# Attention in front of a mixture of experts: the gate weights' cast, the copies out of shared PSUM banks, the offsets' loads and batch 1's v and scaling are placed anew

## The chip, the core and the metric

The kernel runs on one core of a Trainium2 chip. TensorE (PE), VectorE (DVE), ScalarE (ACT), GpSimd (POOL) and SyncE (SP) each take their own instructions in order and wait for one another by semaphores; DMA queues move data between the device memory and the on-chip memories SBUF and PSUM. The metric is the device time of one execution in microseconds (us); the median of the runs counts.

## What is computed

q, k and v have 8 batches, 8 heads, 576 rows and 64 columns. Cut to what matters:

```
q_s = exp(q - max(q, -1)); q_s /= q_s.sum(-1)              # per row
k_s = exp(k - max(k, 2));  k_s /= k_s.sum(2)               # per column, over the sequence
kv  = einsum('bhsd,bhse->bhde', k_s, v)
x   = einsum('bhsd,bhde->bhse', q_s, kv)  -> (4608, 512)    # heads side by side
logits = x @ w_gate + modality_bias[modality_id]           # 8 experts
e   = argmax(logits);  g = softmax(logits)[e]
out[e == i] = g * (relu(x[e == i] @ w1[i]) @ w2[i])        # 512 -> 1024 -> 512
```

With these inputs the modality's bias decides the expert, so each modality has one: two experts, called A and B, are used.

## The kernel before

The program is planned in Python: every piece of work is an `Op` with a cost for each engine that may do it, a rank, and the pieces it depends on. `Plan.order` plays the plan with those costs and writes the instructions in the planned order; each engine then takes its row in that order on the chip, whatever the real times are. `pl.later(o, first)` makes o wait for first in the plan. `Plan.fill` adds unread products (L1498) to PE's row where the plan has PE idle, up to a planned time called `quiet`, until which one PSUM bank is also kept for them.

Batch by batch the attention runs so. SP loads q, k and v into five staging buffers `st` (L414), which are freed by the last work that reads them. ACT takes exp of q (L855) and k (L888), DVE sums q's rows (L861) and inverts the sums (L873), and the scaling (L877, five pieces: four of two column groups and one of one) writes scaled q as bf16 in `eq`; it runs on DVE for batches 0 to 2 and on GpSimd for the others. v is cast to bf16 in two halves (L898): by ACT in batches 0 and 1, by ACT or GpSimd later. PE forms kv in two halves (L990, 18 products each). DVE inverts k's sums (`kinv`, L1017, L1020) and writes the scaled kv as a block diagonal (`kvbd`, L1026, four instructions). PE multiplies scaled q by a permutation (`perm`, L906 on DVE) that sorts rows of the two modalities apart (L1066, 18 products in five groups), ACT or DVE evicts that (`et`, L1078, L1080), and PE multiplies by kvbd (L1105, 20 products in five groups, each group one PSUM bank).

From such a bank the results go to the window of x where A's rows or B's rows stand next: for each 64 rows one copy for A and one for B (L1136, `put`), 18 copies per batch. The windows' offsets are read from `offp` into registers (L1040, a load on each engine that copies). The tuple `copier` says who copies: in batches 0 and 1, A's copies are ACT's and B's are DVE's; in batches 2 and 5 DVE does both, in the others ACT.

When a batch's copies are in place, a pass of A and a pass of B (256 rows each) can run on PE: logits (L1174), first layer (L1241, 32 products of 256 columns, relu by ACT or DVE, L1208, L1210), second layer (L1254, 16 products of 512 columns), gates, `y_sb` (L1214, L1216) and a store by GpSimd (L1219). The logits need the gate weights in bf16, `wg_sb` (L526, cast by DVE from `wg_f`). The experts' weights `W` are loaded by GpSimd's queue (L534, L545) among SP's loads. The rows' places in the output come from comparisons on DVE (`hhi` L725, twelve of `hlo` L713), products of digits on GpSimd (`hv` L737, six) and 36 products on PE (L754), read by DVE as `lst` and `idx` (L766, L768). Copies from batch 3 on wait for those 36 products, since they overwrite their operands.

Of the kernel before, what the change touches and what calls it, by code (L numbers as in the profile page):

```python
# [16 lines left out]
ACT = mybir.ActivationFunctionType  # L17
# [202 lines left out]
def on_act(n):  # L220
    return {"ACT": (0.065 + n / 1200, 0.27 + n / 1200)}


def on_dve(n, rate=1, port=False):
    return {"DVE": (0.065 + n / 960 / rate, 0.28 + n / 960 / rate, port)}


def on_pool(n, per=1.0):
    return {"POOL": (0.07 + n * per / 1000, 0.2 + n * per / 1000, True)}
# [13 lines left out]
def kernel(  # L243
# [13 lines left out]
    B, H, S, Dh = q.shape  # L257
# [5 lines left out]
    NJ = S // 64  # L263
# [21 lines left out]
    pl = Plan()  # L285
# [152 lines left out]
    def load_batch(b):  # L438
        for nm in "qkv":
            load_one(nm, b)  # L440
# [36 lines left out]
    ahead = next(i for i, x in enumerate(transfers) if isinstance(x, str))  # L477
    for b in transfers[:ahead]:
        load_batch(b)
    l_wg = pl.op({"DMA": (0.4, 3.5)}, load_wg, rank=0)  # L480


    key = sb([P, 2], FP32, "key")
# [24 lines left out]
    def experts(_):  # L508
# [16 lines left out]
    wg_c = pl.op(  # L525
        on_dve(32), lambda _: nc.vector.tensor_copy(out=wg_sb, in_=wg_f), [l_wg, c_dve2], rank=11  # L526
    )
# [299 lines left out]
    final, edge, scaled_q = [], {}, []  # L827
# [7 lines left out]
        )  # L835

    started = {"a": False, "b": False}
    filled, perms = {}, []

    copier = [("ACT", "DVE")] * 2 + [(e, e) for e in ("DVE", "ACT", "ACT", "DVE", "ACT", "ACT")]  # L840

    def attention(b):
# [3 lines left out]
        R = 10.0 * b  # L846
# [79 lines left out]
        for (h, n), e in zip(halves, eqx):  # L926
# [5 lines left out]
                    rank=R + 1,  # L932
# [4 lines left out]
        for h, n in halves:  # L937
# [5 lines left out]
                    rank=R + 2,  # L943
# [5 lines left out]
        nq = []  # L949
        for j0, n in groups:  # L950
            n_ = n * HG * Dh
            ncost = on_pool(n_, 1.88)
            if b <= 2:
                ncost = on_dve(n_, 1, True)
            nq.append(
                pl.op(
                    ncost,
                    norm_q(j0, n),
                    [iq] + nq[:1],
                    rank=R + 1,  # L960
                    takes=[] if nq else [eqb],
                    uses=[eqb, qib, bq] if nq else [qib, bq],
                )
            )
# [2 lines left out]
            for o in (o_slot, o_bsel):  # L967
                pl.later(o, nq[-1])
        vcost = {**on_act(S * 2), **on_pool(S * 2, 0.95)}
        if b < 2:  # L970
            vcost = on_act(S * 2)
        cv = []
        for hp in range(2):
# [5 lines left out]
                    rank=R + 0.5,  # L979
# [21 lines left out]
        for hp in range(2):  # L1001
# [5 lines left out]
                    rank=R + 2,  # L1007
# [25 lines left out]
        o_ki = pl.op({"DVE": (0.45, 0.55)}, kinv_run, kvo, rank=R + 2, takes=[kib], uses=kvp)  # L1033
        o_kb = pl.op({"DVE": (1.24, 1.4)}, kvbd_run, [o_ki, c_pool2], rank=R + 2, takes=[kvb], uses=[*kvp, kib])

        ets, win, firsts = [], [], []
        av = {}

        def load_off(e):
# [8 lines left out]

        los = [
            pl.op(  # L1050
                {e: (1.2 if e == "ACT" else 0.6, 1.3)},
                load_off,
                [o_off] + filled.get(b - 2, [])[-2:],
                rank=R + (2.2 if b == 1 else 0.2),
            )
            for e in dict.fromkeys(copier[b])
        ]
        for gi, (j0, nj) in enumerate(groups):
            sbuf = Buf(r_ps)
            w = nj * 64  # L1060
# [13 lines left out]
            def ev(e, j0=j0, nj=nj, sbuf=sbuf):  # L1074
# [11 lines left out]
                rank=R + 3,  # L1086
# [9 lines left out]
                rank=R + 3,  # L1096
# [3 lines left out]
        for gi, (j0, nj) in enumerate(groups):  # L1100
            xbuf = Buf(r_ps)

            def s2(_, j0=j0, nj=nj, xbuf=xbuf):
# [13 lines left out]
                rank=R + 4,  # L1117
# [4 lines left out]
            for jj in range(nj):  # L1122
                for side in range(2):

                    def put(e, jj=jj, j0=j0, nj=nj, side=side, xbuf=xbuf):
# [19 lines left out]
                        if b == B - 1:  # L1145
# [1 line left out]

                    before = win[-2] if len(win) > 1 else filled[b - 1][side - 2] if b else None

                    across = win[-1 - 2 * side] if j0 + jj == NJ - 1 else None  # L1150
                    same = before and before.costs.keys() == {copier[b][side]}
                    win.append(
                        pl.op(
                            on_dve(256) if copier[b][side] == "DVE" else on_act(256),
                            put,
                            [o3, o_id if b >= 3 else None, *los, None if same else before, across],
                            rank=R + 4,
# [2 lines left out]
                    )  # L1160
                    if same:
                        pl.follow(win[-1], before)
        filled[b] = win


    L = sb([P, NSL, E], FP32, "L")
# [319 lines left out]
    for b in range(B):  # L1486
        attention(b)
# [3 lines left out]
        gs = [ffn(side, *p, rank=2.0 * i + side) for side, p in enumerate((pa, pb))]  # L1491
    ffn_rest(gs, 2.0 * i + 0.7)

    quiet = 32.0

    def unread(_):

# [158 lines left out]
```

## Time and profile before

| | us |
|---|---|
| median of 3 runs | 201.58 |
| lowest, highest | 200.18, 202.13 |
| profiled execution | 200.07 |
| its span, first to last instruction | 198.4 |

The profiled execution has 1.67 us around its span. Times below are from the span's start. In a timeline row the first number is the start, the second the time until the last of the merged instructions ended; what stands in brackets is idle time of the engine ahead of it, and what ended it.

### The profile page before, as it was taken

To read this page: it belongs to the slowest core of one execution; us is meant where nothing else is said; L and a number is where in the kernel's file an instruction comes from. 1 tells how busy PE (TensorE), PEld (TensorE's weight loads), DVE (VectorE), ACT (ScalarE), POOL (GpSimd) and SP (SyncE) were. 2 spreads that over 40 slices of the span, in tenths; PEclk is the share of its full clock that TensorE was granted. 3 is DMA by queue.
4 is the path that set the end of the run, shared out by engine and by line. 5 is a ranking of instruction groups with operands and counts; after the bars stand their busy time and mean duration, and the time that the engine had idled before them with its cause. 6 is when DMAs were issued, how large, how long until landed. Compare 5 with 4: busy or idle time off the path is not lost.

```text
span 198.4 us, 5000 instructions
## 1 busy us (share of the span) xinstructions
PE 181.1 (91%) x1757; PEld 123.9 (62%) x1757; DVE 152.3 (77%) x406; ACT 124.5 (63%) x246; POOL 94.8 (48%) x119
## 2 busy tenths in 40 slices
PE   0979986789999999999999999999899999999970
PEld 0435474457596666758685867586757756766740
DVE  3879998789999997958878999856788656655750
ACT  2765889679494786999998996699898000000000
POOL 7089303944540369598496329893112311331241
PEclk9999999699999999999999999999999999999998
DMA  5999999999999999998979941120202102211202
GB/s 189 355 280 259 390 294 247 397 287 211 212 336 407 399 389 340 295 377 267 386 288 280 398 165 55 56 109 0 109 0 107 76 33 106 106 56 53 96 32 90
DMA packets 18588, 42.33 MB, mean 213 GB/s; under 512 B 1913, under 2 KB 1913, under 8 KB 18562
## 3 DMA queue, kind: packets, MB, share of 16 engines
q1 hardware_dynamic: 13344, 28.33, 40.2%
q0 software_dynamic: 5200, 13.64, 23.8%
q8 instruction: 14, 0.23, 0.4%
q14 instruction: 12, 0.10, 0.1%
q10 hardware_dynamic: 18, 0.04, 0.1%
HBM read 36.75 MB, written 9.70 MB: 234 GB/s over the span
## 4 chain that ended last, share of the span: by engine, by line
PE 58%; DVE 17%; ACT 8%; issue 4%; DMA 4%; SPq 3%; POOL 2%; DVEq 1%; ACTq 0%
PE ps L1254 24%; PE ps L1241 23%; DVE xs L1136 5%; ACT xs L1136 4%; DMA wg_f<-in_moe_w_gate_dram 4%; PE ps L990 3%; DVE eq L877 3%; DVE xs L713 3%; PE ps L1105 2%; PE ps L1066 2%; SPq L414 2%; DVE kvbd L1026 2%; PE ps L1174 2%; DVE own L861 1%; POOL eq L877 1%
## 5 line engine op out<-in xcount | busy, mean ns | idle before, releaser
L1241 PE MATMUL ps<-xs,W 128*128 128x256 bf16 x576 | 68.3, 273 | 0.0
L1254 PE MATMUL ps<-W,hT 128*128 128x512 bf16 (+1 forms) x296 | 67.2, 378 | 0.0
L1219 POOL DMA_INDIRECT out_dram<-y_sb,idx x36 | 36.1, 1002 | 59.1 <-DVE y_sb L1216 31.8
L1241 PEld LDWEIGHTS <-W 128*128 128x128 bf16 x576 | 54.9, 98 | 8.4
L1254 PEld LDWEIGHTS <-hT 128*128 128x128 bf16 x296 | 28.5, 99 | 29.1 <-issue 1.4
L1136 ACT CAST xs<-ps 128x256 f32 (+1 forms) x90 | 29.7, 430 | 6.2 <-DVE xs L1136 3.8
L1210 DVE TENSOR_SCALAR hT<-ps 128x512 bf16<-128x512 f32 x41 | 27.9, 689 | 7.1 <-PE ps L1241 5.6
L1216 DVE TENSOR_SCALAR y_sb<-ps,gate 128x512 f32<-128x512 f32 (+1 forms) x26 | 18.9, 729 | 18.3 <-PE ps L1254 13.9
L877 POOL TENSOR_TENSOR eq<-st,qi 128x512 bf16<-128x512 f32 (+1 forms) x25 | 23.8, 979 | 5.6 <-ACT xs L1136 2.9
L861 DVE TENSOR_REDUCE own<-st 128x18 f32<-128x1152 f32 x16 | 21.7, 1354 | 0.7 <-ACT st L855 0.4
L1136 DVE CAST xs<-ps 128x256 f32 (+1 forms) x54 | 19.9, 419 | 2.9 <-ACT xs L1136 1.9
L1208 ACT ACTIVATE hT<-ps 128x512 bf16<-128x512 f32 x33 | 19.1, 604 | 4.0 <-PE ps L1241 2.8
L1078 ACT CAST et<-ps 128x512 bf16<-128x512 f32 (+1 forms) x32 | 16.1, 552 | 6.1 <-PE ps L1066 6.1
L855 ACT ACTIVATE st<-st 128x1152 f32<-128x1152 f32 x16 | 18.4, 1165 | 2.3 <-DMA st<-in_q_dram 2.3
L888 ACT ACTIVATE ek<-st 128x1152 bf16<-128x1152 f32 x16 | 18.5, 1168 | 1.7 <-DMA st<-in_k_dram 1.3
L898 POOL CAST vb<-st 128x1152 bf16<-128x1152 f32 x10 | 11.2, 1145 | 11.4 <-DMA st<-in_v_dram 10.9
L1498 PE MATMUL ps<-ones 128*128 128x512 bf16 x57 | 15.3, 407 | 0.0
L1066 PE MATMUL ps<-perm,eq 128*128 128x128 bf16 x144 | 12.7, 220 | 0.2 <-POOL eq L877 0.2
L990 PE MATMUL ps<-vb,ek 64*128 64x129 bf16 x288 | 11.0, 217 | 1.9 <-ACT vb L898 1.8
L990 PEld LDWEIGHTS <-ek 64*128 64x128 bf16 x288 | 8.3, 93 | 7.0 <-ACT vb L898 2.8
L1105 PE MATMUL ps<-et,kvbd 128*128 128x128 bf16 (+1 forms) x160 | 10.8, 221 | 1.7 <-DVE kvbd L1026 1.7
L1105 PEld LDWEIGHTS <-kvbd 128*128 128x128 bf16 x160 | 9.9, 102 | 3.3 <-DVE kvbd L1026 2.0
(134 smaller groups left out, 170.8 us busy)
## 6 DMA issues: line engine op xcount, KB each, us to landing
st<-in_q_dram SPq DMA_DIRECT2D x6, 1152.0 KB, 7.7
st<-in_k_dram SPq DMA_DIRECT2D x6, 1152.0 KB, 9.8
st<-in_v_dram SPq DMA_DIRECT2D x6, 1152.0 KB, 12.4
st<-in_q_dram SPq DMA_DIRECT2D x4, 576.0 KB, 5.1
st<-in_k_dram SPq DMA_DIRECT2D x4, 576.0 KB, 7.0
st<-in_v_dram SPq DMA_DIRECT2D x4, 576.0 KB, 9.6
W<-in_moe_w_dram POOLq DMA_DIRECT2D x8, 256.0 KB, 6.6
W<-in_moe_w_dram POOLq DMA_DIRECT2D x4, 512.0 KB, 10.6
```

The costliest lines, as they stand in the source:

```text
L861: nc.vector.tensor_reduce(out=sums[qib.idx][:, h * NJ : (h + n) * NJ], in_=view(st[bq.idx], [[Dh, n * NJ], [1, Dh]], h * NJ * Dh), op=ALU.add,
L877: (nc.vector if e == "DVE" else nc.gpsimd).tensor_tensor(out=view(eq[eqb.idx], [[HG * Dh, n], [Dh, HG], [1, Dh]], j0 * HG * Dh), in0=view( ...
L888: nc.scalar.activation(out=view(ek[ekb.idx], [[Dh, n], [HG * Dh, NJ], [1, Dh]], h * Dh), in_=view(st[bk.idx], [[NJ * Dh, n], [Dh, NJ], [1, ...
L990: nc.tensor.matmul(out=ps_t[kvp[hg].idx][:, 130 * hp : 130 * hp + 129], lhsT=ek[ekb.idx][rows, j, P * hp : P * hp + P], rhs=vb[vbb.idx][ro ...
L1105: nc.tensor.matmul(out=view(ps_t[xbuf.idx], [[1, nj * 64]], c * nj * 64), lhsT=kvbd[kvb.idx][:, c, :], rhs=et[etb.idx][:, c, j0 * 64 : (j0 ...
L1136: w_ = nc.scalar.copy(out=dst, in_=src) if e == "ACT" else nc.vector.tensor_copy(out=dst, in_=src)
L1208: nc.scalar.activation(out=dst, in_=src, func=ACT.Relu)
L1210: nc.vector.tensor_scalar_max(out=dst, in0=src, scalar1=0.0)
L1216: nc.vector.tensor_scalar(out=dst, in0=src, scalar1=g, scalar2=None, op0=ALU.mult)
L1219: s_ = nc.gpsimd.indirect_dma_start(out=out, out_offset=bass.IndirectOffsetOnAxis(ap=ix[:, c : c + 1], axis=0), in_=ysb, in_offset=None, b ...
L1241: m = nc.tensor.matmul(out=t[:, i * w : (i + 1) * w], lhsT=w1(W[:, slot_, :], kd, f), rhs=xs[:, kd, lo : lo + w], start=(kd == 0), stop=(k ...
L1254: nc.tensor.matmul(out=t, lhsT=h[:, kf, i * P : (i + 1) * P], rhs=W[:, slot_, W2 + kf * D + c0 : W2 + kf * D + c0 + cn], start=(kf == 0), ...
```

## The change

The cast of the gate weights is placed behind batch 0's last scaling. The planned costs of a copy by two engines are new (`copy_cost`). In a bank that two engines read, B's copies wait in the plan for A's last copy. The last A copy of a batch no longer waits for B's copy before it, but in the last batch. Batch 1's scaling goes to GpSimd, and its v may be cast by GpSimd. The loads of the offsets stand later in batches 0 and 1, batch 1's permutation behind batch 0's kvbd, and `quiet` is 40 instead of 32. The load of the gate weights is written at another place, with the same order of SP's instructions.

```diff
@@
-            if b <= 2:
+            if b in (0, 2):
                 ncost = on_dve(n_, 1, True)
@@
         vcost = {**on_act(S * 2), **on_pool(S * 2, 0.95)}
-        if b < 2:
+        if b < 1:
             vcost = on_act(S * 2)
@@
-                {e: (1.2 if e == "ACT" else 0.6, 1.3)},
+                {e: (1.2 if e == "ACT" else 0.85, 1.3)},
                 load_off,
                 [o_off] + filled.get(b - 2, [])[-2:],
-                rank=R + (2.2 if b == 1 else 0.2),
+                rank=R + (2.2 if b < 2 else 0.2),
@@
+        if not b:
+            for o in los:
+                pl.later(o, nq[-1] if "DVE" in o.costs else cv[-1])
@@
-                    across = win[-1 - 2 * side] if j0 + jj == NJ - 1 else None
+                    across = win[-1 - 2 * side] if j0 + jj == NJ - 1 and b == B - 1 else None
@@
-                            on_dve(256) if copier[b][side] == "DVE" else on_act(256),
+                            copy_cost(copier[b], side),
@@
+            if copier[b][0] != copier[b][1]:
+
+                for o in win[-2 * nj + 1 :: 2]:
+                    pl.later(o, win[-2])
         filled[b] = win
+        if not b:
+            pl.later(wg_c, scaled_q[0])
+        if b == 1:
+            pl.later(perms[1], kvbds[0])
+            for o in los:
+                pl.later(o, filled[0][-1])
@@
-    quiet = 32.0
+    quiet = 40.0
```

`copy_cost` gives (0.46, 0.65) for DVE and (0.4, 0.55) for ACT where the two engines differ, and the old costs elsewhere.

DVE's row in batch 0, from the inverse of q's sums to kvbd (the lines `ok` are small checks that the compiler spreads). Before:

```order
L873 RECIPROCAL qi_86<-qi_86 128x36
L526 CAST wg_sb<-wg_f 128x32
L1535 TENSOR_SCALAR ok<-aoff 1x1
L877 TENSOR_TENSOR eq_70<-st_63,qi_86 128x512 x4
L877 TENSOR_TENSOR eq_70<-st_63,qi_86 128x256
L1017 TENSOR_SCALAR kinv_88<-ps_93 128x2
```

And now, where L881 is the inverse, L885 the scaling, L1025 and L1028 kinv, L1049 the load of the offsets and L527 the cast:

```order
L885 TENSOR_TENSOR eq_70<-st_63,qi_86 128x512 x4
L885 TENSOR_TENSOR eq_70<-st_63,qi_86 128x256
L1025 TENSOR_SCALAR kinv_88<-ps_93 128x2
L1025 TENSOR_SCALAR kinv_88<-ps_94 128x2
L1557 TENSOR_SCALAR ok<-aoff 1x1
L1560 TENSOR_SCALAR ok<-aoff 1x1
L1028 RECIPROCAL kinv_88<-kinv_88 128x4
L1049 TENSOR_LOAD offp
L1034 TENSOR_TENSOR kvbd_74<-ps_93,kinv_88 64x2x64 x2
L1034 TENSOR_TENSOR kvbd_74<-ps_94,kinv_88 64x2x64 x2
L527 CAST wg_sb<-wg_f 128x32
```

The cast went from ahead of the scaling to behind kvbd; the load of the offsets, which stood ahead of the inverse, now stands between kinv and kvbd.

GpSimd's row in batch 1, behind the issue of A's second-layer weights. Before:

```order
L545 DMA W<-in_moe_w_dram 128x2x1024
L737 TENSOR_TENSOR hv<-hhi,vals 128x432 x6
L534 ISA
L534 DMA W<-in_moe_w_dram 64x2x1024
L534 ISA
```

And now, with L906 the casts of v and L885 the scaling of batch 1, L738 hv and L535 the issue of B's weights:

```order
L546 DMA W<-in_moe_w_dram 128x2x1024
L906 CAST vb_73<-st_64 128x2x9x64 x2
L885 TENSOR_TENSOR eq_71<-st_66,qi_87 128x512 x4
L885 TENSOR_TENSOR eq_71<-st_66,qi_87 128x256
L738 TENSOR_TENSOR hv<-hhi,vals 128x432 x4
L535 ISA
```

Seven instructions of batch 1 went in front of hv and of the issue of B's weights, and two of the six hv behind that issue.

GpSimd's row at the last two batches: casts of v of batch 7 (`vb_73`), stores, scaling of batch 6 (`eq_70`) and batch 7 (`eq_71`). Before:

```order
L898 CAST vb_73<-st_65 128x2x9x64 x2
L1219 DMA out_dram<-y_sb_82,idx 4608x512
L877 TENSOR_TENSOR eq_70<-st_66,qi_86 128x512 x2
L1219 DMA out_dram<-y_sb_83,idx 4608x512
L877 TENSOR_TENSOR eq_70<-st_66,qi_86 128x512 x2
L877 TENSOR_TENSOR eq_70<-st_66,qi_86 128x256
```

And now:

```order
L906 CAST vb_73<-st_65 128x2x9x64 x2
L885 TENSOR_TENSOR eq_70<-st_66,qi_86 128x512 x2
L1241 DMA out_dram<-y_sb_82,idx 4608x512
L885 TENSOR_TENSOR eq_70<-st_66,qi_86 128x512
L1241 DMA out_dram<-y_sb_83,idx 4608x512
L885 TENSOR_TENSOR eq_70<-st_66,qi_86 128x512
```

The store ahead of batch 6's scaling moved behind its first two pieces.

## Rows read from the trace of the kernel before

**Rows 1.** The chain that ended last, in order of time: start, us, what.

```profile
66.39 0.36 PE ps L1174 x8
...
155.91 3.49 PE ps L1241 x32
```

**Rows 2.** Timeline, batch 0.

```profile
13.31 0.36 DVE L873 RECIPROCAL qi<-qi 128x36 f32<-128x36 f32 x1
...
14.96 0.22 DVE L526 CAST wg_sb<-wg_f 128x32 bf16<-128x32 f32 x1 [1.28 <-DMA wg_f<-in_moe_w_gate_dram]
...
15.16 2.81 DVE L877 TENSOR_TENSOR eq<-st,qi 128x512 bf16<-128x512 f32 x5
15.17 0.69 PE L990 MATMUL ps<-vb,ek 64*128 64x129 bf16 x18
...
18.15 1.67 PE L1498 MATMUL ps<-ones 128*128 128x512 bf16 x7
...
18.42 1.21 DVE L1026 TENSOR_TENSOR kvbd<-ps,kinv 64x128 bf16<-64x128 f32 x4
...
19.66 1.17 PE L1105 MATMUL ps<-et,kvbd 128*128 128x128 bf16 x20
...
20.08 3.22 ACT L1136 CAST xs<-ps 128x256 bf16<-128x256 f32 x8 [1.10 <-PE ps L1105]
...
25.48 0.37 ACT L1136 CAST xs<-ps 128x256 f32 x1 [1.13 <-DVE xs L1136]
```

**Rows 3.** The line of the offsets' loads: duration in ns min/median/max, first and last start.

```profile
L1040 DVEq TENSOR_LOAD <-offp x4: 849/1180/1203, 11.9 to 86.4; - x4
```

**Rows 4.** Timeline, batches 1 and 2.

```profile
18.73 0.97 SPq L414 DMA_DIRECT2D st<-in_v_dram  x2
...
30.01 2.22 DVE L877 TENSOR_TENSOR eq<-st,qi 128x512 bf16<-128x512 f32 x4
...
31.89 1.18 ACT L898 CAST vb<-st 128x1152 bf16<-128x1152 f32 x1
...
35.38 0.29 PE L1105 MATMUL ps<-et,kvbd 128*128 128x128 bf16 x2 [1.36 <-DVE kvbd L1026]
...
37.25 0.79 ACT L1136 CAST xs<-ps 128x256 f32 x2 [0.49 <-DVE xs L1136]
...
42.60 5.65 DVE L713 TENSOR_TENSOR xs<-own,lo 128x384 bf16<-128x384 f32 x12
42.74 0.82 PE L1174 MATMUL ps<-wg_sb,xs 128*128 128x8 bf16 x16 [0.55 <-DVE xs L1136]
...
46.91 1.24 PE L754 MATMUL ps<-hv,xs 128*128 128x72 bf16 x33
...
49.44 0.18 DVE L766 COPY lst<-ps 128x36 f32<-128x36 f32 x1
...
60.39 6.27 DVE L1136 CAST xs<-ps 128x256 f32 x18
```

**Rows 5.** The page's DMA issues: count, KB each, median us to landing.

```profile
st<-in_v_dram SPq DMA_DIRECT2D x4, 576.0 KB, 9.6
```

**Rows 6.** GpSimd's scaling, 60 to 120 us: duration in ns min/median/max.

```profile
L877 POOL TENSOR_TENSOR eq<-st,qi x15: 626/1063/1086, 71.2 to 104.2; 128x512 bf16<-128x512 f32 x12, 128x256 bf16<-128x256 f32 x3
```

**Rows 7.** Timeline, batches 4 to 7.

```profile
88.73 1.17 ACT L898 CAST vb<-st 128x1152 bf16<-128x1152 f32 x1
...
89.95 0.37 SPq L414 DMA_DIRECT2D st<-in_q_dram  x1
...
117.69 2.24 POOL L898 CAST vb<-st 128x1152 bf16<-128x1152 f32 x2 [6.11 <-DMA st<-in_v_dram]
...
122.53 0.39 PE L1066 MATMUL ps<-perm,eq 128*128 128x128 bf16 x4
...
143.66 0.96 PE L1174 MATMUL ps<-wg_sb,xs 128*128 128x8 bf16 x32 [0.67 <-ACT xs L1136]
```

**Rows 8.** Windows: stretch, length, PE, PEld, DVE, ACT, POOL busy, granted clock, DMA.

```profile
36.25:39.67 3.42, 3.42 (x23) 2.05 (x21) 2.13 (x8) 1.88 (x5) 3.42 (x6) 0.50 1.04 393
```

More of the change, by code (lines that the diff above doesn't have):

```diff
@@ L479 @@
         load_batch(b)
-    l_wg = pl.op({"DMA": (0.4, 3.5)}, load_wg, rank=0)
+        if not b:
+            l_wg = pl.op({"DMA": (0.4, 3.5)}, load_wg, rank=0)
     key = sb([P, 2], FP32, "key")
@@ L837, with copy_cost @@
     started = {"a": False, "b": False}
-    filled, perms = {}, []
+    filled, perms, kvbds = {}, [], []
+    def copy_cost(engines, side):
+        apart = engines[0] != engines[1]
+        if engines[side] == "DVE":
+            return {"DVE": (0.46, 0.65)} if apart else on_dve(256)
+        return {"ACT": (0.4, 0.55)} if apart else on_act(256)
     copier = [("ACT", "DVE")] * 2 + [(e, e) for e in ("DVE", "ACT", "ACT", "DVE", "ACT", "ACT")]
@@ L1034, in attention @@
         o_kb = pl.op({"DVE": (1.24, 1.4)}, kvbd_run, [o_ki, c_pool2], rank=R + 2, takes=[kvb], uses=[*kvp, kib])
+        kvbds.append(o_kb)
         ets, win, firsts = [], [], []
@@ L1162, in attention @@
                         pl.follow(win[-1], before)
+            if copier[b][0] != copier[b][1]:
+                for o in win[-2 * nj + 1 :: 2]:
+                    pl.later(o, win[-2])
         filled[b] = win
+        if not b:
+            pl.later(wg_c, scaled_q[0])
[3 more added lines that the diff above has]
+                pl.later(o, filled[0][-1])
     L = sb([P, NSL, E], FP32, "L")
```

## Prediction

> **What bounds the kernel now.** I read the chain of waits first, from its end backwards. From 66.39 us on it is PE: first-layer and second-layer products of the experts without a gap worth naming [rows 1], up to one wait at 143.66, where PE stands 0.67 for ACT's last copy of batch 7 [rows 7]. So behind 66.39 the time is PE's amount of work; what can be won lies ahead of it, in what makes the logits of batch 2 start at 66.39. There the chain runs over DVE: the 18 copies of batch 2 from 60.39 [rows 4], behind batch 2's scaling, behind the places (lst, 49.44), which wait for PE's 36 products of digits (from 46.91), for twelve DVE comparisons (42.60 to 48.25) and for batch 1's copies. The timeline of batch 0 [rows 2] shows what the change aims at: DVE stands 1.28 us for the gate weights with its scaling queued behind, and ACT's ninth copy stands 1.13 us for DVE.
>
> **Gate cast behind batch 0's scaling.** The reciprocal ends at 13.67, so the scaling could start at 13.70 instead of 15.16 and end at 16.5 instead of 17.97: 1.46 on DVE. What is late next? DVE's load of the offsets now stands between the reciprocal and kvbd, where nothing hides it: 0.85 to 1.20 us [rows 3]. Before it lay behind perm and cost nothing. kvbd took from 18.42 to 19.63; with 0.45 from scaling to kvbd and the load it now ends at 18.8 to 19.3. But PE takes its row in order: the second half of kv can't start before ACT's cast of v (15.17), ends near 15.8, and ahead of the first kvbd product stand 18 products of scaled q (0.055 each, half of the 0.109 that 3.49 / 32 gives for 256 columns [rows 1]: 1.0) and now 14 unread fill products (ten before; both counted in the order) at 0.216 (1.51 from 18.15 to 19.66, by seven): 3.0. That is 19.8, against 19.66. The win is eaten by the fill: 0, or +0.1.
>
> **A ahead of B in a bank.** In batch 0, ACT's copies take 0.40 (3.22 by eight). Nine without the wait for DVE end near 23.8, not 25.85. With 16 fill products behind the kvbd products PE can start A's first pass at 24.2, over 1 us sooner; but next in line is batch 1, which hangs on its v, so by itself this is worth 0. In batch 1 the engines took turns on each bank, copy by copy (ACT at 37.25 had waited 0.49 for DVE [rows 4]): now two A copies go while DVE takes the bank before. That shortens the copying from some 6.4 us to nine copies of 0.44 and two of A's, if the products come as fast.
>
> **Batch 1 on GpSimd.** They don't. v was issued at 18.73; the median from issue to landing is 9.6 us [rows 5], so 28.8 for the second half by that estimate, and 31.89 at the latest, when ACT cast it without waiting for it. I take 30.4. GpSimd casts at 1.12 a half (2.24 by two [rows 7]): done at 31.6, where ACT was done at 33.07, so kv comes 1.5 us sooner. But the scaling stands behind the casts on GpSimd: four of 1.06 and one of 0.63 [rows 6] end at 36.5, where DVE ended at 32.23 [rows 4]: 4.3 later. PE's row is now woven to that pace: two groups' kvbd products behind the third scaled group (34.8), then A's second layer in two halves of 1.73 (eight of 512 columns, each like a fill product's 0.216) between the others. Counting on: 35.5, 36.3, 38.1, 38.4, 40.1, 40.3; ACT's second y copy, then A's ninth copy, 41.4; seven fill products end at 41.8. The logits of batch 1 start there, against 42.74: -0.9.
>
> Against it stands the clock. PE now idles some 2 us between kv's halves (29.7 to 31.7). Before, it idled 1.36 us ahead of the kvbd products (until 35.38), and the granted clock was at its lower level (0.50, 1.2 GHz) from 36.25 to 39.67 [rows 8]. If it now falls while PE runs the scaled-q products and six fill products, those take double: +1.0, logits at 42.8. The Trainium skill, page "TensorE: Matmul & The Clock Gate", section "What's actually happening", says the array's clock is one of two levels, set by how busy the array has lately been. By that rule alone I'd count the fall as certain, and the stage as worth +0.1. The trace agrees so far as its one fall stands behind such a gap. But seven fill products now lie around the gap, where only four lay before: I take the middle, -0.4 (range -0.9 to +0.1).
>
> **Comparisons woven in.** Five of DVE's twelve comparisons now stand between batch 1's copies, seven behind them: 7 x 0.47 = 3.3 (5.65 by 12 [rows 4]). B's ninth copy near 42.3 puts their end at 45.6, not 48.25, so the digits no longer wait for DVE, only for PE: 42.3 + 0.4 + 3.5 (A's pass) + 1.3 = 47.5. GpSimd's part: hv, four behind the scaling, then the issue of B's weights (about 2 us later than before, behind transfers that still run then), then two: near 45.7, hidden. lst at 47.6 against 49.44: -1.8. Of this 0.7 is given back: one relu of 0.65 now stands on DVE ahead of batch 2's copies. So the logits of batch 2 start at 65.3 rather than 66.39: **-1.1** (range -1.6 to -0.5). Offsets loaded on ACT lie behind its cast of v: 0.
>
> **Behind 66.** PE's work is the same. After the last kvbd products 24 first-layer and 16 second-layer products (6.1) now cover batch 7's copies instead of 32 first-layer ones (3.5): the 0.67 at 143.66 goes, take -0.6. On the other side PE's row asks for batch 6's scaled q sooner: behind its first products there now stand one more kv half (0.62) and 24 more first-layer products (2.62), 3.2 in all. Before they started at 122.53; now PE is there at 122.53 - 1.1 - 3.2 = 118.2. GpSimd still casts v of batch 7 first, for which it waited 6.11 us, until 117.69 [rows 7]; with 2.24 for the casts and 1.06 for the first group (a store that stood between is gone) it would be ready at 121.0. So 2.8 are lost unless v lands sooner. It should: the load of batch 6's q was issued at 89.95, when ACT had cast v of batch 4 (88.73 to 89.90 [rows 7]); that cast is now GpSimd's, right behind the first scaled group of batch 4, no longer behind ACT's 18 copies of batch 3, and the loads behind it wait for buffers one after the other. No row prices that; it lies between nothing and all of the 2.8, and I take 2.0 as regained: +0.8, range 0 to 2.8.
>
> **Sum**: -1.1 - 0.6 + 0.8 = -0.9 on the profiled execution's 200.07 us (span 198.4, 1.67 around it), so 199.2, or 0.45% less. The median of the three runs shown is 201.58; the same ratio gives 200.7.
>
> **Rivals.** (A) Clock and loads both turn out well: the clock holds, v of batch 7 lands 3 us sooner. -1.6 - 0.67 = -2.3: 197.8, as a median 199.3; a little more if PE, now with fill until a planned 40 us, also avoids the half clock's cost elsewhere. For it: the cast of batch 4 that went from ACT to GpSimd no longer stands among ACT's copies. (B) Slower, by GpSimd at the end: v of batch 7 lands no sooner but 1.5 us later, because casts of v that ACT did before now queue behind scalings and stores on GpSimd, and each staging buffer frees later. Then PE stands 2.8 + 1.5 at batch 6's scaled q: -1.1 - 0.6 + 4.3 = +2.6: 202.7, as a median 204.2. It decides from a landing later than about 116: below, the change is at worst neutral. For it: GpSimd's casts grow from 10 to 12 and it gets the five scalings of batch 1; against it: it idled 6.11 us there. (C) The change doesn't reach the path: fill products and v's landing hold batches 0 and 1 where they were, the clock falls, the relu eats the comparisons' win: 0, 201.6.
>
> **How the numbers follow.** Three runs of one kernel spread by 1%, so 1% is about what a measurement of this kernel can tell from no change. Forecast and (C), both within 1%: 0.45, of which the forecast 0.33. (A) 0.32 and other gains 0.03: faster 0.35. (B) 0.17 and other losses 0.03: slower 0.20. The range goes to 197.6 below (A with a further 0.8%) and 203.9 above, just short of (B).
>
> **What would show it.** In the changed profile: scaling of batch 0 near 13.7; first kvbd product still near 19.8, straight behind fill; ACT's ninth copy of batch 0 without a wait; GpSimd's five scalings of batch 1 between 31.6 and 36.5; lst near 47.6; logits of batch 2 near 65.3; GpSimd's casts of v of batch 7 near 115, and PE waiting or not for the first scaled group of batch 6. The forecast is wrong if PE's row gaps in places that I count as full between 66 and 143, since the whole order there is new.

## The result, and the profile after

| | before | after |
|---|---|---|
| median, us | 201.09 (20 runs) | 198.35 (20 runs) |
| lowest, highest | 199.71, 202.97 | 197.06, 202.26 |
| profiled execution, its span | 200.07, 198.4 | 198.34, 196.8 |

The ratio is 0.9859, 95% interval 0.9834 to 0.9884: 1.4% less, where the forecast was 0.45% (200.7 on a median of 201.58) and the range 197.6 to 203.9. Ratios, here and below, are taken over the runs within 1.5% of the fastest of their kernel, so a median over all runs can stand apart from them.

The two profiles differ by 1.73 us, the medians by 2.74. The first profile of before was one of its quick executions, that of after lies on its median; so before was profiled once more (first experiment).

Busy time of each engine and the chain that ended last, from the page of the changed kernel:

```profile
PE 183.0 (93%) x1769; PEld 125.8 (64%) x1769; DVE 150.6 (77%) x403; ACT 120.8 (61%) x242; POOL 100.3 (51%) x126
...
PE 72%; DMA 9%; DVE 5%; ACT 4%; issue 3%; POOL 2%; SPq 1%; DVEq 0%; POOLq 0%; ACTq 0%
```

The chain now runs over PE and transfers; DVE has 5% of it, against 17% before. What its early part hangs on has changed as well. Two pieces of the chain of before (start, us, what):

```profile
7.08 7.75 DMA wg_f<-in_moe_w_gate_dram
...
32.02 1.05 ACT vb L898
```

And two of the chain of after:

```profile
19.38 8.48 DMA st<-in_v_dram
...
30.84 1.14 POOL vb L906
```

Before, the chain led from the transfer of the gate weights over DVE's row and then ACT's row to the cast of batch 1's v. Now it leads over the transfer of that v itself. The timeline of batch 0 after the change, against [rows 2]:

```profile
13.92 3.01 DVE L885 TENSOR_TENSOR eq<-st,qi 128x512 bf16<-128x512 f32 x5
...
18.54 1.22 DVE L1034 TENSOR_TENSOR kvbd<-ps,kinv 64x128 bf16<-64x128 f32 x4 [1.27 <-POOL bsel L705]
...
19.33 0.28 PE L1117 MATMUL ps<-et,kvbd 128*128 128x128 bf16 x2
...
19.81 1.07 PE L1117 MATMUL ps<-et,kvbd 128*128 128x128 bf16 x18 [0.21 <-DVE kvbd L1034]
20.14 3.62 ACT L1148 CAST xs<-ps 128x256 bf16<-128x256 f32 x9 [1.92 <-PE ps L1117]
...
24.18 0.35 PE L1196 MATMUL ps<-wg_sb,xs 128*128 128x8 bf16 x8
```

The scaling starts at 13.92, and ahead of kvbd DVE is idle for 1.27: that is the offsets' load, which the timeline does not count as busy. (The releaser named there had long been done.) The first kvbd product stands where it stood. ACT's nine copies run without a wait, and A's logits come at 24.18 instead of 25.45.

Batches 1 and 2, against [rows 4, 6]:

```profile
30.82 1.15 POOL L906 CAST vb<-st 128x1152 bf16<-128x1152 f32 x1 [1.77 <-DMA st<-in_v_dram]
31.94 4.70 POOL L885 TENSOR_TENSOR eq<-st,qi 128x512 bf16<-128x512 f32 x5
32.03 1.16 PE L998 MATMUL ps<-vb,ek 64*128 64x129 bf16 x18 [1.48 <-POOL vb L906]
...
36.20 0.61 PE L1117 MATMUL ps<-et,kvbd 128*128 128x128 bf16 x8
...
42.67 0.34 PE L1196 MATMUL ps<-wg_sb,xs 128*128 128x8 bf16 x8
...
47.94 0.20 DVE L767 COPY lst<-ps 128x36 f32<-128x36 f32 x1 [0.24 <-PE ps L755]
...
59.31 0.69 DVE L1232 TENSOR_SCALAR hT<-ps 128x512 bf16<-128x512 f32 x1 [0.17 <-PE ps L1263]
59.91 6.05 DVE L1148 CAST xs<-ps 128x256 f32 x18
...
65.68 0.36 PE L1196 MATMUL ps<-wg_sb,xs 128*128 128x8 bf16 x8 [0.21 <-issue]
```

Windows over the start of batch 1's kv, PE alone (length, PE busy, granted clock, DMA share, GB/s), against [rows 8]:

```profile
32.00:34.00 2.00, 1.97 (x24) 0.50 0.81 157
34.00:36.00 2.00, 2.00 (x13) 0.76 0.98 373
```

PE stood 1.48 for the cast, and the clock was at its lower level (0.50, 1.2 GHz) right behind. Batches 6 and 7, against [rows 7]:

```profile
84.23 0.37 SPq L414 DMA_DIRECT2D st<-in_q_dram  x1
...
114.17 2.24 POOL L906 CAST vb<-st 128x1152 bf16<-128x1152 f32 x2 [0.33 <-issue]
...
118.89 0.39 PE L1078 MATMUL ps<-perm,eq 128*128 128x128 bf16 x4
...
139.57 0.96 PE L1196 MATMUL ps<-wg_sb,xs 128*128 128x8 bf16 x32
```

GpSimd's wait of 6.11 for v of batch 7 is gone, PE has no wait at batch 6's scaled q, and none ahead of the last logits.

### The profile page after: what moved, and what is told of

Read it like the earlier page. It is cut to its first block, busy times and chain, and to the rows that moved or that the text cites. A ratio compares the mean times of both kernels' runs of the same rounds, so it can differ in the third digit from the quotient of the medians.

```text
span 196.8 us, 5031 instructions
## 1 busy us (share of the span) xinstructions
PE 183.0 (93%) x1769; PEld 125.8 (64%) x1769; DVE 150.6 (77%) x403; ACT 120.8 (61%) x242; POOL 100.3 (51%) x126
## 4 chain that ended last, share of the span: by engine, by line
PE 72%; DMA 9%; DVE 5%; ACT 4%; issue 3%; POOL 2%; SPq 1%; DVEq 0%; POOLq 0%; ACTq 0%
PE ps L1276 28%; PE ps L1263 27%; DMA st<-in_v_dram 4%; PE ps L998 4%; PE ps L1078 3%; PE ps L1117 3%; DMA W<-in_moe_w_dram 3%; DMA st<-in_q_dram 2%; PE ps L1520 2%; ACT xs L1148 2%; PE ps L1196 2%; SPq L414 1%; DVE own L869 1%; POOL vb L906 1%; DVE xs L1148 1%
## 5 line engine op out<-in xcount | busy, mean ns | idle before, releaser
L1276 PE MATMUL ps<-W,hT 128*128 128x512 bf16 (+1 forms) x296 | 66.1, 373 | 0.0
L1232 DVE TENSOR_SCALAR hT<-ps 128x512 bf16<-128x512 f32 x44 | 30.0, 689 | 6.0 <-PE ps L1263 4.0
L1238 DVE TENSOR_SCALAR y_sb<-ps,gate 128x512 f32<-128x512 f32 (+1 forms) x23 | 16.7, 727 | 18.0 <-PE ps L1276 15.5
L885 POOL TENSOR_TENSOR eq<-st,qi 128x512 bf16<-128x512 f32 (+1 forms) x30 | 28.4, 972 | 1.6 <-PE ps L1263 1.3
L1230 ACT ACTIVATE hT<-ps 128x512 bf16<-128x512 f32 x30 | 18.1, 627 | 4.7 <-issue 1.9
L1520 PE MATMUL ps<-ones 128*128 128x512 bf16 x69 | 20.2, 432 | 0.0
L896 ACT ACTIVATE ek<-st 128x1152 bf16<-128x1152 f32 x16 | 18.8, 1186 | 1.0 <-DMA st<-in_k_dram 1.0
L906 POOL CAST vb<-st 128x1152 bf16<-128x1152 f32 x12 | 13.6, 1150 | 7.1 <-DMA st<-in_v_dram 6.4
L1078 PE MATMUL ps<-perm,eq 128*128 128x128 bf16 x144 | 13.4, 222 | 0.1
L1236 ACT ACTIVATE y_sb<-ps,gate 128x512 f32<-128x512 f32 x14 | 9.8, 698 | 5.3 <-PE ps L1276 4.2
L1078 PEld LDWEIGHTS <-eq 128*128 128x128 bf16 x144 | 10.2, 99 | 4.4 <-issue 1.1
```

The source lines that it names most:

```text
L885: (nc.vector if e == "DVE" else nc.gpsimd).tensor_tensor(out=view(eq[eqb.idx], [[HG * Dh, n], [Dh, HG], [1, Dh]], j0 * HG * Dh), in0=view( ...
L896: nc.scalar.activation(out=view(ek[ekb.idx], [[Dh, n], [HG * Dh, NJ], [1, Dh]], h * Dh), in_=view(st[bk.idx], [[NJ * Dh, n], [Dh, NJ], [1, ...
L1078: nc.tensor.matmul(out=view(t, [[2 * nj * 64, 2], [1, 64]], hp * nj * 64 + jj * 64), lhsT=eq[eqb.idx][:, j0 + jj, P * hp : P * hp + P], rh ...
L1232: nc.vector.tensor_scalar_max(out=dst, in0=src, scalar1=0.0)
L1276: nc.tensor.matmul(out=t, lhsT=h[:, kf, i * P : (i + 1) * P], rhs=W[:, slot_, W2 + kf * D + c0 : W2 + kf * D + c0 + cn], start=(kf == 0), ...
L1520: nc.tensor.matmul(out=ps_t[n_ps - 1], lhsT=ones, rhs=view(ones, [[0, 4], [1, P]]), start=True, stop=True)
```

## The experiments

The planner reorders everything behind an edit of its costs, so the edits here don't touch the plan's rules. Each kernel takes the finished list of pieces (of before or of after), moves a few of them or gives them to another engine, and then writes all in that order; the numbers are places in the list. Names that begin with b_ are made from before, with a_ from after. Four starts that the readings below rest on, and the span, one profiled execution each:

| kernel | A's first logits | cast of v, batch 1, second half | logits, batch 1 | logits, batch 2 | span |
|---|---|---|---|---|---|
| before | 25.45 | 31.89 | 42.74 | 66.39 | 198.4 |
| b_again | 26.08 | 32.52 | 43.38 | 67.04 | 199.4 |
| b_tail | 24.94 | 31.38 | 42.24 | 66.60 | 198.2 |
| after | 24.18 | 30.82 | 42.67 | 65.68 | 196.8 |
| a_cast_back | 26.23 | 32.96 | 45.13 | 67.92 | 198.5 |
| a_hlo_back | 24.63 | 31.28 | 43.45 | 68.08 | 198.6 |
| a_b1_dve | 23.94 | 31.36 | 43.51 | 67.65 | 198.4 |
| a_v4_act | 25.70 | 31.48 | 42.63 | 70.33 | 201.8 |
| a_clock | 24.83 | 31.31 | 42.46 | 69.41 | 200.0 |
| a_v2 | 24.08 | 29.60 | 40.75 | 64.14 | 195.1 |
| a_v2_dve | 23.96 | 30.52 | 41.67 | 64.73 | 195.9 |
| a_v2_pe | 23.34 | 30.99 | 42.93 | 66.94 | 198.5 |
| a_v2_both | 24.50 | 30.57 | 40.60 | 64.44 | 196.0 |

**b_again: before, unchanged.**

> The kernel before, unchanged, profiled once more. Its first profile took 200.07 us, the median of its twenty timed runs is 201.09, so the difference of the two profiles (1.73) is a third smaller than that of the medians (2.74). My theory: between runs of one kernel it is the landing of the loads of batches 0 to 2 that varies, the rows behind 66 us keep their distances, and a slower run of before starts the logits of batch 2 later than 66.39 by about what its span is longer than 198.4. Rival: the stretch behind 66 us varies (waits at batch 6's scaled q or ahead of the last logits).

Measured: 200.98, on the median of before. From its timeline, ACT and PE:

```profile
26.08 0.81 PE L1174 MATMUL ps<-wg_sb,xs 128*128 128x8 bf16 x16 [0.95 <-DVE xs L1136]
26.12 0.37 ACT L1136 CAST xs<-ps 128x256 f32 x1 [1.12 <-DVE xs L1136]
26.39 1.17 ACT L855 ACTIVATE st<-st 128x1152 f32<-128x1152 f32 x1
...
30.04 1.08 ACT L1208 ACTIVATE hT<-ps 128x512 bf16<-128x512 f32 x2
30.99 1.17 ACT L898 CAST vb<-st 128x1152 bf16<-128x1152 f32 x1
32.03 0.63 ACT L1208 ACTIVATE hT<-ps 128x512 bf16<-128x512 f32 x1
32.52 1.18 ACT L898 CAST vb<-st 128x1152 bf16<-128x1152 f32 x1
...
33.76 0.69 PE L990 MATMUL ps<-vb,ek 64*128 64x129 bf16 x18
...
144.63 0.95 PE L1174 MATMUL ps<-wg_sb,xs 128*128 128x8 bf16 x32 [0.68 <-ACT xs L1136]
```

The reader is to see that ACT's row has no gap from its ninth copy to the second cast of v, and that the cast waits for no transfer. In the three profiles of before's early order the cast stands 6.44 us behind A's first logits each time (31.89 - 25.45, 32.52 - 26.08, 31.38 - 24.94). So it is not v's landing that starts batch 1's kv in before, but ACT's row behind A's logits. And what moves A's logits is the landing of the gate weights: DVE's scaling of batch 0, right behind their cast, starts at 15.16, 15.79 and 14.65 in these three profiles, and A's logits come 10.29 behind it each time. So my theory was right that a landing varies, though it is not one of q, k or v. It held for two thirds of the difference: the logits of batch 2 come 0.65 later of a span 0.97 longer; another 0.3 lies behind them, around batch 6's scaled q (123 to 128 us).

**b_tail: before, 8 second-layer products ahead of the last logits.**

```diff
+plan.insert(818, plan.pop(825))   # 8 products (825) ahead of batch 7's 32 logits (818)
```

> The kernel before in its own frozen order, with one move: the first 8 of the 16 second-layer products that stood behind batch 7's 32 logits stand ahead of them. My theory, from the term of 0.6 for this wait: the 8 products (1.73 us) cover ACT's last copy, PE's wait of 0.67 us goes, nothing behind it is late, so 0.6 to 0.7 us less (0.3%). Rival: the end of the kernel is set by a chain behind PE (DVE's relus, the stores) that has its own slack to lose, so the wait comes back in another place: 0.

Measured: ratio 0.9977 (0.9940 to 1.0014), by the middle 0.46 us, with an interval that reaches beyond zero. The timeline shows the wait gone:

```profile
143.41 1.89 PE L1254 MATMUL ps<-W,hT 128*128 128x512 bf16 x8
145.13 0.95 PE L1174 MATMUL ps<-wg_sb,xs 128*128 128x8 bf16 x32
```

From the logits of batch 2 to the span's end it takes 131.56, against 132.04 and 132.35 in the two profiles of before. So the term is right in sign and size (0.5 to 0.8), though the timing alone would not prove it.

This profile shows one thing more. Its batch 1's logits came 0.50 sooner than in before, but its batch 2's logits 0.21 later:

```profile
42.24 0.82 PE L1174 MATMUL ps<-wg_sb,xs 128*128 128x8 bf16 x16 [2.21 <-DVE xs L1136]
42.92 5.32 PE L1241 MATMUL ps<-xs,W 128*128 128x256 bf16 x32
```

The window of PE behind that wait (length, PE busy, granted clock, DMA share, GB/s):

```profile
44.00:46.00 2.00, 2.00 (x13) 0.55 1.13 214
```

PE had stood 2.21 for DVE's copies, the clock was near its lower level (0.55) behind it, and the 32 first-layer products took 5.32 instead of the 3.65 of before. So in before the landing of the gate weights reached batch 1's logits in all three profiles, but batch 2's logits in two only.

**a_cast_back: the gate cast ahead of batch 0's scaling again.**

```diff
+plan.insert(56, plan.pop(88))     # wg_c (88) ahead of batch 0's first scaling (56)
```

> The changed kernel in its own frozen order, with the cast of the gate weights put back ahead of batch 0's scaling on DVE. My theory, that this part of the change is worth nothing because v of batch 1 is next: the scaling starts near 15.2 instead of 13.9, the first kvbd product near 20.8 instead of 19.8, A's first pass near 25.5 instead of 24.4, and kv of batch 1 still at 32.0; time within 0.3 us. Rival, that the wait of 1.28 us on DVE counted: slower by 1.0 to 1.4 us.

Measured: ratio 0.9841 (0.9777 to 0.9904), the same as after's 0.9859; the interval ends 0.9 us above it, so it only just excludes the rival's 1.0 to 1.4. The profiled execution (200.16 us, against a median of 197.81) caught the gate weights late:

```profile
15.86 0.18 DVE L527 CAST wg_sb<-wg_f 128x32 bf16<-128x32 f32 x1 [2.40 <-DMA wg_f<-in_moe_w_gate_dram]
...
20.60 1.21 DVE L1034 TENSOR_TENSOR kvbd<-ps,kinv 64x128 bf16<-64x128 f32 x4 [0.85 <-DVE kinv L1028]
...
26.23 0.35 PE L1196 MATMUL ps<-wg_sb,xs 128*128 128x8 bf16 x8
...
32.96 1.15 POOL L906 CAST vb<-st 128x1152 bf16<-128x1152 f32 x1 [2.90 <-DMA st<-in_v_dram]
```

DVE waits 2.40, A's logits come 2.05 later than in after, and GpSimd still stands 2.90 for v, which was issued when it is in after (19.34 against 19.38) and landed 2.1 later. So in the changed kernel what is won or lost in batch 0 ends at v's landing.

**a_hlo_back: the comparisons behind batch 1's copies.**

```diff
+back = [plan[i] for i in (205, 210, 215, 223, 234)]   # five comparisons
+plan[249:249] = back                                  # behind the last copy (248)
+for i in (234, 223, 215, 210, 205): plan.pop(i)
```

> The changed kernel in its own frozen order, with the five comparisons that stand between batch 1's copies on DVE put behind the last of these copies, so that all twelve follow it as before. My theory, by which the weaving was worth 1.8 us at lst: lst near 49.5 instead of 47.94, PE stands 1.3 to 1.6 us in front of the digits (it had no wait there), the logits of batch 2 near 67.2 instead of 65.68, the whole 1.3 to 1.8 us slower. Rival: batch 1's copies end sooner on DVE without the comparisons between them, which pays for them, and PE's other work hides the rest: 0 to +0.4.

Measured: ratio 0.9941 (0.9898 to 0.9983), 0.8% more than after's, some 1.65 us. Timeline:

```profile
43.58 5.66 DVE L714 TENSOR_TENSOR xs<-own,lo 128x384 bf16<-128x384 f32 x12
...
50.70 0.18 DVE L767 COPY lst<-ps 128x36 f32<-128x36 f32 x1
...
68.08 0.36 PE L1196 MATMUL ps<-wg_sb,xs 128*128 128x8 bf16 x8 [0.85 <-ACT st L863]
```

From the logits of batch 1 to lst it takes 7.25 (50.70 - 43.45) against 5.27 in after, and to the logits of batch 2 24.63 against 23.01: the weaving is worth 1.6. PE does not lose 1.3 to 1.6 at the digits, as I had it: its 36 products of digits take 2.21 there (47.35 to 49.56), against 1.33 in after, so 0.9, and at batch 2's logits it stands 0.85 instead of 0.21, another 0.6.

**a_b1_dve: batch 1's scaling by DVE, its casts by GpSimd.**

```diff
+nq1 = [plan[i] for i in (170, 179, 186, 195, 206)]    # the five scalings
+for i in (206, 195, 186, 179, 170): plan.pop(i).engine = "DVE"
+plan[167:167] = nq1                                   # behind the reciprocal (166)
```

> The changed kernel in its own frozen order, with batch 1's five scalings on DVE right behind its reciprocal, while GpSimd keeps both casts of v. My theory: DVE stood idle for 2.4 us ahead of kinv of batch 1, so the scaling (about 3.3 us) nearly fits there; the first kvbd product of batch 1 no longer keeps step with GpSimd (36.20) and goes to 35.5, the logits of batch 1 from 42.67 to about 42.0, and the time falls by 0 to 0.7 us: the scaling on GpSimd was no gain, the casts were. Rival, that the scaling on GpSimd is what gained: DVE's comparisons and places come 1 us later, lst near 49, 0.5 to 1.5 us slower.

Measured: ratio 0.9924 (0.9882 to 0.9965), by the middle 1.3 us slower than after, with intervals that just touch: the rival's number, but not by its reason. lst stands 5.26 behind the logits of batch 1, as in after. In the profile, 0.84 of the loss lies ahead of batch 1's logits: v of batch 1 was cast 0.54 later, and from that cast to the logits it takes 12.15 instead of 11.85. The first kvbd product stands at 37.04, not at 35.5. Another 1.13 lies between the logits of batch 1 and those of batch 2, where v of batch 2 is late:

```profile
39.83 0.66 POOL L535 DMA_DIRECT2D W<-in_moe_w_dram  x1 [2.33 <-DMA st<-in_q_dram]
...
48.99 1.15 ACT L906 CAST vb<-st 128x1152 bf16<-128x1152 f32 x1 [1.33 <-DMA st<-in_v_dram]
...
50.69 0.61 PE L1276 MATMUL ps<-W,hT 128*128 128x512 bf16 x2 [0.66 <-ACT hT L1230]
```

GpSimd, without the scaling, is free early, waits for q of batch 2 and issues B's weights when q has landed. v of batch 2, issued at 32.66, is cast only at 48.99; ACT stands 1.33 for it with a relu queued behind, and PE 0.66 for that relu. Why v was late is not shown: after issues the same weights at 40.04, only 0.21 later, and there v is in time (last section).

**a_v4_act: v of batch 4, second half, by ACT again.**

```diff
+plan[484].engine = "ACT"
+plan.insert(493, plan.pop(484))   # behind ACT's 18 copies of batch 3
```

> The changed kernel in its own frozen order, with the second half of v of batch 4 cast by ACT behind its 18 copies of batch 3, as before, instead of by GpSimd. My theory of the term of +0.8 (range 0 to 2.8): this cast frees the buffer that the load of batch 6's q waits for, so that load is issued near 89 instead of 84.2, and what follows it comes later in turn; GpSimd waits for v of batch 7 again and PE stands 0.5 to 2 us at batch 6's scaled q: 0.5 to 2 us slower. Rival: the later loads are held by other buffers or by the transfers themselves, v of batch 7 is issued at 104.9 in either case, and the time is the same within 0.3 us.

Measured: ratio 0.9855 (0.9807 to 0.9903), the same as after; the interval leaves room for a loss of up to 0.9 us. Rows:

```profile
91.80 0.37 SPq L414 DMA_DIRECT2D st<-in_q_dram  x1
...
110.59 0.37 SPq L414 DMA_DIRECT2D st<-in_v_dram  x1
...
119.89 2.23 POOL L906 CAST vb<-st 128x1152 bf16<-128x1152 f32 x2 [1.21 <-DMA st<-in_v_dram]
```

This execution took 203.39 us, the longest of its six, since its batch 2 was 4.65 late (70.33 against 65.68). Counted from its logits, the load of batch 6's q is 2.9 later than in after, but v of batch 7, five loads on, only 1.0 (110.59 - 70.33 against 104.92 - 65.68): the loads catch up. GpSimd waits 1.21 for it, and PE has no wait at batch 6's scaled q (it stands 0.85 at batch 4's kv for the moved cast itself, which the timing can't tell). My theory fell: with 2.9 lost at batch 6's q, v of batch 7 was still cast in time for PE.

**a_clock: ten more unread products around kv of batch 1.**

```diff
+plan[176:176] = [plan[15]] * 7    # ahead of kv's second half
+plan[164:164] = [plan[15]] * 3    # ahead of its first
```

> The changed kernel in its own frozen order, with ten more unread products on PE while it waits for v of batch 1: three ahead of kv's first half, seven ahead of its second. My theory: the granted clock stays at 1.0 from 31.5 to 35, where it was 0.5; the first kvbd product of batch 1 comes at about 35.6 instead of 36.20 (GpSimd's scaling is then the pace) and the logits of batch 1 at about 42.2 instead of 42.67, 0.3 to 0.6 us less in all. Rival 1: the clock falls as before, 0. Rival 2: DVE's copies of batch 2 hold the logits of batch 2 at 65.7 whatever PE does before, so the gain turns into PE's wait there: 0.

Measured: ratio 0.9852 (0.9808 to 0.9897), the same; the interval is wider than the 0.3 to 0.6 us that I expected. The window of PE:

```profile
34.00:36.00 2.00, 2.00 (x20) 1.00 0.85 208
```

The clock holds, and from the cast of v to the logits of batch 1 it takes 11.15 instead of 11.85. In this execution (201.54 us, against a median of 199.12) v of batch 2 was late, which hides what follows:

```profile
50.74 1.15 ACT L906 CAST vb<-st 128x1152 bf16<-128x1152 f32 x1 [4.12 <-DMA st<-in_v_dram]
...
52.44 0.61 PE L1276 MATMUL ps<-W,hT 128*128 128x512 bf16 x2 [3.29 <-ACT hT L1230]
```

**a_yswap: the second layer's second half in place of seven unread products.**

```diff
+plan[249:256] = [plan[228]]       # 8 products for 7 unread ones
+plan.insert(246, plan.pop(241))   # ACT's scaling of their result
+plan.pop(228)
```

> The changed kernel in its own frozen order, with the second 8 products of A's second layer (1.73 us) in the place of the seven unread products (1.51 us) that stood in front of batch 1's logits; ACT scales their result behind A's ninth copy. My theory, that from 42.67 on PE's amount of work sets the end: PE stands about 0.8 us for ACT in front of batch 1's last kvbd product, its logits come near 42.1 with no work left over from before, 0.4 to 0.7 us less in all. Rival: the chain over DVE to batch 2's copies sets the time, PE then waits at 65.7: 0.

Measured: 201.39, ratio 1.0004. It says nothing: I had put ACT's scaling ahead of the products that it reads, so it takes what the bank held before, one tile of the output is stale, and PE then waits 2.86 us for it, for nothing. a_v2_pe is the mended form.

**a_v2, a_v2_dve, a_v2_pe, a_v2_both: two profiles showed ACT standing 4.1 us for v of batch 2, so its cast goes to GpSimd; then less work on DVE ahead of batch 2, a shorter way on PE to batch 1's logits, and both.**

```diff
+at = list(plan)                                # move(x, y): piece x right behind piece y
+at[280].engine = "POOL"; move(295, 299)        # all four: cast of v; kv behind the second layer
+at[346].engine = "ACT"; move(339, 380)         # _dve, _both: a relu, perm of batch 3
+del plan[249:256]                              # _pe, _both: the seven unread products
+move(228, 238); move(227, 244); move(241, 246) # second layer's half behind kvbd's products
+for x, bank in ((238, 3), (256, 5), (258, 1)): at[x].takes[0].idx = bank
```

> The changed kernel in its own frozen order, with two moves: the first half of v of batch 2 is cast by GpSimd, where ACT cast it between two relus, and PE takes kv's first half of batch 2 behind both halves of the second layer instead of between them. My theory: the changed kernel has a wait that its first profile doesn't show and two profiles of its variants do (ACT 4.1 us for v of batch 2 with relus queued behind, PE 3.3 us for them), so its runs spread from 197.1 to 202.3; without it the slowest runs fall below 200.5, the fastest stay at 197, the median falls by 0.3 to 0.8 us (ratio to before 0.982 to 0.984). Rival: v of batch 2 landing late costs the same whoever casts it: spread and ratio (0.986) stay.

> As the run with v of batch 2 cast by GpSimd, and two operations taken from DVE ahead of batch 2's copies: one relu (0.69 us) goes to ACT, perm of batch 3 (1.36) behind the copies. My theory, that PE's amount of work from 42.67 on sets the end and its only wait before 66 in the changed kernel is 0.21 us: the copies start 2 us sooner, the logits of batch 2 only 0.2 sooner; 0 to 0.2 us less than without the two. Rival, that DVE's chain to batch 2's copies still sets the time, as in the kernel before: 1.5 to 2 us less.

> As the run with v of batch 2 cast by GpSimd, and PE's way to batch 1's logits made 1.5 us shorter: no unread products ahead of them, the second layer's second half behind the last kvbd products, ACT's scaling of it behind A's ninth copy. My theory, that PE and DVE are balanced there: batch 1's logits near 41.6 instead of 42.67, but PE then waits for the comparisons at the digits and for batch 2's copies at 65.5, since DVE has no idle time from 33 to 66; 0 to 0.3 us less. Rival, that PE's work alone sets the end: 0.9 to 1.1 us less.

> Both edits, of PE's row ahead of batch 1's logits and of DVE's ahead of batch 2's copies, on top of v of batch 2 cast by GpSimd. My theory (PE and DVE balanced up to 66): together 0.5 to 1.0 us less than v of batch 2 by GpSimd alone, more than the sum of the two single edits, with the logits of batch 2 near 64.8. Rival: the loads of batch 1 and 2 set both, and nothing comes sooner: 0.

Measured, as ratios to before: 0.9915 (0.9878 to 0.9951), 0.9869 (0.9829 to 0.9909), 0.9885 (0.9834 to 0.9936), 0.9879 (0.9832 to 0.9926). None is better than after's 0.9859; a_v2 is by the middle 1.1 us slower, with intervals that just touch, and why stays open. a_v2 ran from 196.68 to 201.22, nearly as wide as after: the theory of the spread fell, and since its profile (span 195.1) is of its shortest execution, what the longer ones wait for stays open. The profiles tell more of the other two questions. Batch 2's copies and logits in a_v2_dve:

```profile
58.95 6.06 DVE L1148 CAST xs<-ps 128x256 f32 x18 [1.84 <-PE ps L1117]
...
64.73 0.36 PE L1196 MATMUL ps<-wg_sb,xs 128*128 128x8 bf16 x8
```

With 2 us less in front, DVE now stands 1.84 for PE and PE does not stand for DVE. From the cast of v it is 34.21 to the logits of batch 2, against 34.54 in a_v2: in these two executions the 2 us were worth 0.3, near my theory. By the runs a_v2_dve is 0.9 us ahead of a_v2, with intervals that overlap, so they don't decide between theory and rival. In a_v2_pe the clock fell behind a wait of 2.45, and from the cast to batch 1's logits it takes 11.94, so its profile doesn't show what the shorter way on PE is worth. In a_v2_both the way from the cast to batch 1's logits is 10.03, 1.1 shorter than a_v2's 11.15, and to batch 2's 33.87, 0.7 shorter; the logits of batch 2 at 64.44 are close to the 64.8 expected, but the runs don't show it.

## Why the prediction was off by 1%

**Ahead of 66: the rows after the change came close, the account of before did not.** Row by row the forecast of the changed kernel holds within 0.4 us: A's logits at 24.18 (24.2 forecast), the end of the second cast of v at 31.97 (31.6), the logits of batch 1 at 42.67 (42.3), lst at 47.94 (47.6), the logits of batch 2 at 65.68 (65.3). Their gain was forecast as -1.1; it is -0.71 against the quick profile of before and -1.36 against the one on its median.

- *Gate cast and bank order, each worth 0.* For the first, a_cast_back shows it in the changed kernel, although the load of the offsets took 1.27 and not 0.85 to 1.20 (kvbd ended at 19.76, and it, not the fill, released most of the first products, at 19.81). By the prediction's own terms kvbd's end comes to 19.0 to 19.4 (16.5, 0.45, the load, 1.21), not to 18.8 to 19.3. But in before both sat on the path: the chain leads from the gate weights' transfer to the cast of v. I wrote that batch 1 "hangs on its v" and had seen that the cast at 31.89 did not wait for it; what it did wait for was ACT's row, tied to A's logits by 6.44. With the cast on GpSimd the tie is gone. What the bank order alone would give in before was not run; I estimate up to the 1.13 of ACT's wait, since ACT's row has no gap behind it.
- *kv 1.5 sooner by GpSimd's casts.* The cast that ended at 33.07 ends at 31.97: 1.1 sooner. It starts when v lands: in the ten profiles of after and its variants in the table between 29.60 and 32.96, with a wait for the transfer in every one. v's landing is where the early stage now starts.
- *The clock, -0.9 to +0.1.* It held in five of those ten profiles (11.15 from the cast to batch 1's logits in the four whose PE row there is after's, one of them with a_clock's added products) and fell in the other five (11.85 to 12.17 in the four with after's PE row). In the three profiles of before's order this way took 10.85 to 10.86, whether the clock fell there (before, b_again) or not (b_tail): DVE's copies set it, not PE. So GpSimd's pace costs 0.3 and the fall another 0.7 to 1.0, about the +1.0 of the prediction. Between the profiled executions batch 1's logits moved by -0.07, inside the forecast range of -0.9 to +0.1. The Trainium skill, page "TensorE: Matmul & The Clock Gate", section "What's actually happening", makes the level depend on how busy the array has lately been. The five falls agree in that PE had stood 1.48 to 2.50 ahead of the kv half. But the clock also held behind 1.47 (a_v2_both) and 1.69 (a_v2_dve), so idle time just ahead doesn't decide alone, and the fall that the prediction called certain by that rule is not.
- *Comparisons -1.8, of which 0.7 is given back.* lst moved by 1.50; counted from batch 1's logits, 6.70 became 5.27. From lst to batch 2's logits 16.95 became 17.74: 0.79 given back. a_hlo_back confirms 1.6 for the weaving as a whole.

**Behind 66: the step that failed.** I had -0.6 for the wait at 143.66 and +0.8 for PE asking for batch 6's scaled q before v of batch 7 lands, +0.2 in all. Measured from the logits of batch 2 to the end: 132.04 and 132.35 before, 131.08 after (the spans to two digits are 198.43, 199.39 and 196.76), so -1.0 to -1.3. The wait went, as b_tail's profile shows by itself. The +0.8 is 0: GpSimd casts v of batch 7 at 114.17 with no wait for a transfer. The first scaled group of batch 6 is then ready near 117.6 (half of the 2.08 that two groups take from 116.52), not at 121.0, and PE reaches it at 118.89 (forecast 118.2) without a stop. I had taken 2.0 of 2.8 as regained and charged the rest; in fact the whole is covered. v of batch 7 was issued 2.1 sooner than in before (104.92 against 107.02) and cast 9.25 behind its issue instead of 10.67. a_v4_act shows why the range was too pessimistic: loads held back at batch 6's q have caught up most of it by v of batch 7. Why the transfer itself was shorter stays open.

Of the 1.8 us missed (0.9 forecast, 2.7 measured) this term is 0.8; another 0.4 to 0.7 lies in the rest of this stretch (-1.0 to -1.3 against -0.6) and 0.3 ahead of 66 (-1.36 against -1.1). In the rest of the stretch are small waits of PE between 120 and 130 us, around batch 6's scaled q (0.17 in before, 0.32 in b_again, none in after), which the prediction counted as nothing, and 0.2 less behind the last product.

**The median.** I scaled a quick execution's sum to the median. b_again shows what a median execution of before looks like: the gate weights land later, A's logits come 0.63 later, and ACT's row carries that into batch 1. In after that row no longer ends in kv, so a late batch 0 costs nothing there (a_cast_back), though a late v does. That this is why the medians lie further apart than the first two profiles is read from two profiles of before and not tested by itself. In sum rival (A), 199.3, came nearest, by its tail (v of batch 7 fully hidden), though not by its clock.

## What to carry to other kernels

Before calling an edit worth nothing because a transfer is next, look whether the engine behind that transfer really waited for it: if the distance between two events is the same in every profile (6.44 three times), an engine's row ties them, and the edit counts until the transfer is met. Profile the old kernel until one profile lies on its median; here the first was 1 us quick, as much as the effect forecast. Read the chain of waits from its start as well as from its end: the gate weights' transfer, whose cast I priced at nothing, stood near its head. To price the parts of a change that a planner spreads over the program, freeze the finished order and move single pieces.

## What the runs showed of the hardware

A load of offsets into registers costs its full length where nothing hides it: DVE stood 0.85 (a_cast_back, ahead of kvbd at 20.60) to 1.27 us for it (after), which is the range of DVE's four loads in the changed kernel, 0.85 to 1.28 us.

A fall of TensorE's clock cost time only where PE set the pace. In before's batch 1 the clock was at its lower level from 36.25 to 39.67 [rows 8] and at full in b_tail, yet both took the same time from the cast of v to the logits (10.85 and 10.86), since PE then waited for DVE's copies. In the changed kernel the same way took 11.15 with the clock held and 11.85 to 12.17 with it fallen, and in b_tail a fall behind a wait of 2.21 stretched the first layer from 3.65 to 5.32.

What holds v of batch 2 in some executions stays open. In three of the ten profiles GpSimd stood for q of batch 2 and issued B's weights as soon as it had landed (39.83, 41.62 and 41.77: a_b1_dve, a_v4_act, a_clock). There v of batch 2, issued earlier on another queue, was cast 9.0 to 9.2 us behind that issue, at 48.99 to 50.86, after a wait for it. That looks as if the weights' transfers held v back, but three things speak against reading it so. In these three profiles q itself landed 8.3 to 8.8 us behind its issue, before the weights were issued, and in b_tail, where GpSimd also stood for q, after 6.7. In b_tail the weights followed at once as well (38.30), and v was cast 13.6 behind its own issue, against 15.4 to 16.7 in the three. And after issued the weights only 0.21 later than a_b1_dve and had v in time. No run moved the issue alone.
